# k0 ahead of the sketches, k1 and q1 between the halves of the weights, one outer product on GpSimd

## The chip, the core and the metric

The kernel runs on one core of a Trainium2 chip. A core has a matrix engine (TensorE, PE in the rows), three engines for element work (VectorE = DVE, ScalarE = ACT, GpSimd = POOL), a queue engine (SyncE = SP) that here only sends loads and stores, and 16 DMA engines. Each engine works through its own list of instructions in order; semaphores tie the lists together. The metric is the device time of one execution in microseconds, median over several runs. The list of each engine is exactly the order in which the Python code emits its instructions.

## What is computed

Linear attention with a polynomial feature map, then a feed-forward layer:

```python
def phi(x):                                   # x: (4 batches, 4 heads, 1088 tokens, 32)
    a = np.einsum('rd,bhsd->bhsr', S1, x)     # r = 8
    b = np.einsum('rd,bhsd->bhsr', S2, x)
    return np.einsum('bhsi,bhsj->bhsij', a, b).reshape(*x.shape[:-1], 64)
q_p, k_p = phi(q), phi(k)
kv  = np.einsum('bhsf,bhsd->bhfd', k_p, v)
z   = np.sum(k_p, axis=2)
num = np.einsum('bhsf,bhfd->bhsd', q_p, kv)
den = np.einsum('bhsf,bhf->bhs', q_p, z)[..., None] + 1e-06
x   = (num / den), as 4352 tokens x 128
h   = x @ w_in                                # 128 -> 2048
out = (h * sigmoid(beta * h)) @ w_out         # 2048 -> 128
```

The result is float32, 4352 x 128.

## The kernel before

The four batches go one after another through the attention part, and the feed-forward part is woven between its steps.

**Attention of a batch b.** `turn_k` and `turn_q` (DVE) transpose 32x32 blocks of the loaded k and q into `kT` and `qT`. `kps` (PE) multiplies `kT` by the sketches `sk` into PSUM; two DVE transposes bring that back as `kab`. `outer(b, h)` (DVE, one call per head) forms the 64 features of k in `kp`, out of two inputs in SBUF. `kv` (PE) multiplies `kp` by v and by ones, head by head within each j, into `kvz`; its first part takes j = 1 to 4, the second the rest. `ab` (PE) multiplies `qT` by the two sketches into `aps` and `bps`; ACT copies `aps` to `asb`, DVE multiplies `bps` by it into `qp`. `ndt` transposes `kv` and its sum (`zb`, `nd`). `den` and `num` (PE) give `dps` and `nps`; DVE inverts the denominator (`dT`, `rc`, `rb`) and writes the quotient into `xT`. q is handled in two parts n = 0 and 1 (18 and 16 of 34 blocks).

**Feed-forward.** Nine chunks of 512 tokens (the last of 256), eight waves each: `w1` is two PE products `wave` with `winp` and one ACT activation `g` (Silu) over 1024 columns; `w2` is two products into `moeout` with `woutp`, two waves behind. `winp` = w_in times beta and `woutp` = w_out divided by beta are made by GpSimd, in halves of 1024 columns of d_ff: four `prep_win`, four `prep_wout`, then again. `slot(group, n)` emits a step of attention and behind it n waves. So PE takes the waves and the attention steps in one fixed order: after the first three waves comes `ab` of batch 1 and batch 0 (`r_group((1, 0, 0), (0, 1, 1))`), which needs `qT` of batch 1. `keep_warm(n)` is n products on a tile of ones that no one reads.

**Loads.** Nearly all go through SP's queue in program order: S1, the first half of k0, q0; v0 (held behind the first `turn_k` of batch 0); w_in, beta (spread over the partitions), w_out, each of the first half and then each of the second; then k, q, v of batch 1, of 2, of 3. ACT's queue carries S2, the second half of k0 and a small copy of beta. A load of SP's that takes up a completion semaphore again waits for the load that used it last, so about eight loads are on the way at once.

The lines that matter below: the loads are L82 (S), L94 (k, q), L108 (v), L140, L141, L147 (w_in, beta, w_out); `turn_k` L307, `turn_q` L319, `kab` L341, `kp` L350, `qp` L392, `kvz` L410, `winp` L190, `woutp` L205.

Of the kernel before, what the change touches and what calls it, by code (L numbers as in the profile page):

```python
# [9 lines left out]
F32 = mybir.dt.float32  # L10
# [4 lines left out]
P = 128  # L15
# [3 lines left out]
def kernel(  # L19
# [58 lines left out]

    sr = []
    for n, (s_, eng) in enumerate(((S1, nc.sync), (S2, nc.scalar))):  # L80
        t = const.tile([P, D], F32, tag=f"sr{n}", name=f"sr{n}")
        eng.dma_start(  # L82
            out=t, in_=bass.AP(tensor=s_.tensor, offset=s_.offset, ap=[[0, P // R], [D, R], [1, D]])
        )
        sr.append(t)
# [45 lines left out]
    k_t[0] = load_rows(k, 0, "k", halves)  # L131
    q_t[0] = load_rows(q, 0, "q")
    nc.scalar.dma_start(out=beta_jp, in_=moe_beta.rearrange("(j p) -> j p", p=P))

    def load_rest(gate):
        v_t[0] = load_v(0, gate)
        for c in range(0, DFF, DFF // 2):
            cs = slice(c, c + DFF // 2)
            js = slice(c // P, (c + DFF // 2) // P)
            nc.sync.dma_start(out=w_in_sb[:, cs], in_=moe_w_in[:, cs])  # L140
            nc.sync.dma_start(  # L141
                out=beta_bc[:, cs],
                in_=bass.AP(
                    tensor=moe_beta.tensor, offset=moe_beta.offset + c, ap=[[0, P], [1, DFF // 2]]
                ),
            )
# [179 lines left out]
    def kps(b):  # L326
        t = ps2.tile([P, 2, 512], F32, tag="two", name="kps")
        for g in range(4):
            for pi in range(2):
                rows = slice(64 * pi, 64 * pi + 64)  # L330
                nc.tensor.matmul(  # L331
                    out=t[32 * g : 32 * g + 32, pi, : NJK * 32],
                    lhsT=sk[rows, :],
                    rhs=kT_of[b][rows, KBASE[g] * 32 : (KBASE[g] + NJK) * 32],
                    start=True,
                    stop=True,
                )

        KAB[b] = sbA.tile([P, 2, NJK, 32], F32, tag="kab", name="kab")
        for pi in range(2):  # L340
            nc.vector.transpose(  # L341
                out=KAB[b][:, pi].rearrange("p j c -> p (j c)"), in_=t[:, pi, : NJK * 32]
            )
        KP[b] = sbA.tile([P, H, NJK, F], F32, tag="kp", name="kp")

    def outer(b, h, j0=0, j1=NJK):
# [3 lines left out]
        nc.vector.tensor_tensor(  # L350
# [180 lines left out]


# [67 lines left out]
    for b in range(1, B + 1):  # L600
# [25 lines left out]
        if more:  # L626
            slot(lambda: kps(b + 1), two)
# [50 lines left out]
```

## Time and profile before

| | |
|---|---|
| time, median of 3 runs | 131.19 us (130.79 to 132.09) |
| the profiled execution | 129.78 us, its span 127.7 us |
| PE busy | 110.7 us (87% of the span) |
| ACT busy | 78.9 us (62%) |
| DVE busy | 67.9 us (53%) |
| GpSimd busy | 11.1 us (9%) |
| read from and written to HBM | 10.00 MB and 2.23 MB |
| mean granted clock of PE | 0.986 of full speed |

The span runs from the first to the last instruction of the execution; 2.08 us of its time lie around it. Busy time of PE counts pipelined products, so a busy PE need not be PE at its peak. In rows of the trace, "[0.67 <-DVE kp L350]" is idle time of the engine just before the row, and what ended it; "x8" counts instructions that the row merges.

### The profile page before, as it was taken

What the parts mean: (1) busy time and instruction counts of PE and PEld (TensorE: products, weight loads), DVE (VectorE), ACT (ScalarE), POOL (GpSimd) and SP (SyncE); (2) the same over time, 40 slices, a digit from 0 to 9 for tenths busy, and PEclk for the clock granted to TensorE, in tenths of its full rate; (3) what the DMA queues carried; (4) which work ended last, traced back from release to release, by engine and by line L of the source; (5) the groups of instructions that cost most, each with busy time, mean ns of one, the idle gap of its engine ahead of it and who ended that gap; (6) DMA issues with size and microseconds to landing.
All of it is one profiled execution on the core that took longest, in us unless ns stands there. A gap on an engine that the chain in (4) does not pass through costs nothing.

```text
span 127.7 us, 3100 instructions
## 1 busy us (share of the span) xinstructions
PE 110.7 (87%) x1282; PEld 45.6 (36%) x1282; DVE 67.9 (53%) x134; ACT 78.9 (62%) x96; POOL 11.1 (9%) x24
## 2 busy tenths in 40 slices
PE   5849979529959999969999999999999998989970
PEld 2224513112244423233433433453433343434550
DVE  2579326533892399899476589962449302020120
ACT  2303104704608666438798896688786899999960
POOL 3000399900000000000000000000000000000000
PEclk9999999995999999999999999999999999999999
DMA  2889999999980005000140004005000403203253
GB/s 43 319 187 274 334 354 381 216 308 220 306 185 19 11 9 78 0 0 0 26 63 0 5 10 72 0 5 82 0 5 11 71 0 53 29 6 47 37 79 44
DMA packets 24765, 12.42 MB, mean 97 GB/s; under 512 B 18976, under 2 KB 23088, under 8 KB 24752
## 3 DMA queue, kind: packets, MB, share of 16 engines
q1 hardware_dynamic: 23888, 11.88, 38.3%
q10 hardware_dynamic: 864, 0.35, 1.2%
q8 instruction: 10, 0.16, 0.6%
q14 instruction: 3, 0.02, 0.1%
HBM read 10.00 MB, written 2.23 MB: 96 GB/s over the span
## 4 chain that ended last, share of the span: by engine, by line
PE 45%; ACT 18%; DMA 12%; DVE 11%; SPq 8%; issue 4%; ACTq 0%; DVEq 0%
ACT g L269 17%; PE wave L261 15%; PE moeout L224 13%; DMA q<-in_q_dram 9%; PE kvz L410 4%; PE aps L373 4%; SPq L94 3%; DMA k<-in_k_dram 3%; PE dps L475 2%; PE nps L510 2%; DVE rb L493 2%; PE bps L373 2%; DVE kp L350 2%; PE kps L331 1%; DVE kT L307 1%
## 5 line engine op out<-in xcount | busy, mean ns | idle before, releaser
L269 ACT ACTIVATE g<-wave 128x1024 f16<-128x1024 f32 x68 | 65.5, 1033 | 17.9 <-PE wave L261 17.5
L261 PE MATMUL wave<-xT,winp 128*128 128x512 f16 (+1 forms) x144 | 40.9, 373 | 2.1 <-ACT g L269 1.0
L224 PE MATMUL moeout<-g,woutp 128*128 128x512 f16 (+1 forms) x144 | 39.4, 370 | 0.0
L261 PEld LDWEIGHTS <-winp 128*128 128x128 f16 x144 | 12.2, 97 | 23.5 <-issue 15.5
L224 PEld LDWEIGHTS <-woutp 128*128 128x128 f16 x144 | 14.2, 98 | 15.5 <-issue 0.8
L383 ACT COPY asb<-aps 128x576 f32<-128x576 f32 (+1 forms) x16 | 9.6, 613 | 15.5 <-PE aps L373 13.3
L234 DVE STREAM_TRANSPOSE o_sb<-moeout 128x512 f32<-128x512 f32 (+1 forms) x9 | 6.2, 687 | 23.2 <-PE moeout L224 23.2
L392 DVE TENSOR_TENSOR qp<-bps,asb 128x576 f32<-128x576 f32 (+1 forms) x16 | 11.3, 712 | 13.0 <-PE bps L373 8.7
L373 PE MATMUL aps<-qT,s_135 32*64 32x288 f32 (+1 forms) x128 | 11.3, 412 | 5.5 <-DVE qT L319 5.5
L373 PE MATMUL bps<-qT,s_140 32*64 32x288 f32 (+1 forms) x128 | 11.2, 411 | 0.3 <-ACT asb L383 0.3
L350 DVE TENSOR_TENSOR kp<-kab 128x576 f32<-128x576 f32 (+2 forms) x20 | 11.4, 617 | 0.0
L410 PE MATMUL kvz<-kp,v 128*32 128x64 f32 (+1 forms) x288 | 9.1, 223 | 2.4 <-DVE kp L350 2.4
L163 PE MATMUL warm<-idle 128*128 128x512 f16 x25 | 8.0, 458 | 1.5 <-DVE hm L175 1.5
L410 PEld LDWEIGHTS kvz<-kp,v 128*32 128x32 f32 (+1 forms) x288 | 6.2, 109 | 6.9 <-DVE kp L350 3.5
L373 PEld LDWEIGHTS aps<-qT,s_135 32*64 32x64 f32 x128 | 3.7, 129 | 10.7 <-issue 7.9
L307 DVE STREAM_TRANSPOSE kT<-k 128x1088 f32<-128x1088 f32 (+2 forms) x5 | 5.3, 1073 | 4.0 <-DMA k<-in_k_dram 4.0
L190 POOL TENSOR_TENSOR winp<-w_in_sb,beta_bc 128x256 f16<-128x256 f32 x8 | 5.6, 724 | 13.6 <-DMA beta_bc<-in_moe_beta_dram 13.6
L520 DVE TENSOR_TENSOR xT<-nps,rb 128x576 f16<-128x576 f32 (+1 forms) x8 | 5.8, 722 | 1.2 <-PE nps L510 1.0
L319 DVE STREAM_TRANSPOSE qT<-q 128x576 f32<-128x576 f32 (+1 forms) x8 | 5.8, 726 | 1.0 <-DMA q<-in_q_dram 1.0
L486 DVE STREAM_TRANSPOSE dT<-dps 128x288 f32<-128x288 f32 (+1 forms) x8 | 3.7, 461 | 5.0 <-PE dps L475 5.0
L493 DVE STREAM_TRANSPOSE rb<-rc 128x576 f32<-128x576 f32 (+1 forms) x8 | 6.0, 745 | 0.3
L510 PE MATMUL nps<-qp,nd 64*32 64x288 f32 (+1 forms) x128 | 5.5, 401 | 0.0
(53 smaller groups left out, 57.6 us busy)
## 6 DMA issues: line engine op xcount, KB each, us to landing
v<-in_v_dram SPq DMA_DIRECT2D x16, 144.0 KB, 8.1
q<-in_q_dram SPq DMA_DIRECT2D x4, 544.0 KB, 11.5
k<-in_k_dram SPq DMA_DIRECT2D x3, 544.0 KB, 11.9
out_dram<-o_sb SPq DMA_DIRECT2D x20, 64.0 KB, 2.0
w_in_sb<-in_moe_w_in_dram SPq DMA_DIRECT2D x2, 512.0 KB, 7.6
beta_bc<-in_moe_beta_dram SPq DMA_DIRECT2D x2, 512.0 KB, 8.2
w_out_sb<-in_moe_w_out_dram SPq DMA_DIRECT2D x2, 512.0 KB, 9.9
k<-in_k_dram SPq DMA_DIRECT2D x1, 288.0 KB, 3.7
```

The source lines that it names most:

```text
L163: nc.tensor.matmul(out=t, lhsT=idle[:, :P], rhs=idle, start=True, stop=True)
L224: nc.tensor.matmul(out=moe["acc"][:, :tw], lhsT=woutp[:, j, :], rhs=g[:, jj, :tw], start=(j == 0), stop=(j == NJ - 1),)
L261: nc.tensor.matmul(out=wv[:, jj * tw : (jj + 1) * tw], lhsT=winp[:, (j0 + jj) * P : (j0 + jj + 1) * P], rhs=xT[:, t0 : t0 + tw], start=Tru ...
L269: nc.scalar.activation(out=g, in_=wv, func=ACTF.Silu)
L307: last = nc.vector.transpose(out=kT_of[b][:, 32 * t0 : 32 * t1], in_=k_t[b][:, t0:t1].rearrange("p t d -> p (t d)"),)
L350: nc.vector.tensor_tensor(out=KP[b][:, h, j0:j1].rearrange("p j (i l) -> p j i l", i=R), in0=bass.AP(tensor=a0.tensor, offset=a0.offset, a ...
L373: nc.tensor.matmul(out=dst[64 * c : 64 * c + 64, m, : 32 * tn], lhsT=sx[rows, :], rhs=qT_of[bb][rows, t0 : t0 + tn, c, :], start=True, sto ...
L383: nc.scalar.copy(out=ASB[a_of][:, :, :w], in_=aps[:, :, :w])
L392: nc.vector.tensor_tensor(out=QP[bb][:, 2 * pr : 2 * pr + 2, 32 * t0 : 32 * t0 + w], in0=bps[:, :, :w], in1=ASB[b_of][:, :, :w], op=MUL,)
L410: nc.tensor.matmul(out=kvz[32 * h : 32 * h + 32, F * which : F * which + F], lhsT=v_t[b][:kr, h, j, :] if which == 0 else ones[:kr, :], rh ...
L493: nc.vector.transpose(out=rb[:, :tn].rearrange("p t c s -> p (t c s)"), in_=bass.AP(tensor=r0.tensor, offset=r0.offset, ap=[list(r0.ap[0]) ...
L510: nc.tensor.matmul(out=nps[32 * h : 32 * h + 32, c, :w], lhsT=ND[b][rows, 32 * h : 32 * h + 32], rhs=QP[b][rows, h, 32 * t0 : 32 * t0 + w] ...
```

## The change

**Loads.** The first half of k0 goes ahead of S1 on SP's queue, the second half ahead of S2 on ACT's. In the list of SP's loads k1 stands behind the first half of the weights, q1 behind w_in and beta of the second half, and w_out of the second half behind q1; v1 follows.

SP's queue before, from the first load of the weights to k and q of batch 1 (in the names, `in_..._dram` is the tensor in HBM):

```order
L140 DMA w_in_sb<-in_moe_w_in_dram 128x1024
L141 DMA beta_bc<-in_moe_beta_dram 128x1024
L147 DMA w_out_sb<-in_moe_w_out_dram 128x8x128
L140 DMA w_in_sb<-in_moe_w_in_dram 128x1024
L141 DMA beta_bc<-in_moe_beta_dram 128x1024
L147 DMA w_out_sb<-in_moe_w_out_dram 128x8x128
L94 DMA k<-in_k_dram 128x1088
L94 DMA q<-in_q_dram 128x1088
L108 DMA v<-in_v_dram 32x4x288 x4
```

And the same stretch of SP's queue now:

```order
L140 DMA w_in_sb<-in_moe_w_in_dram 128x1024
L141 DMA beta_bc<-in_moe_beta_dram 128x1024
L147 DMA w_out_sb<-in_moe_w_out_dram 128x8x128
L86 DMA k<-in_k_dram 128x1088
L140 DMA w_in_sb<-in_moe_w_in_dram 128x1024
L141 DMA beta_bc<-in_moe_beta_dram 128x1024
L86 DMA q<-in_q_dram 128x1088
L147 DMA w_out_sb<-in_moe_w_out_dram 128x8x128
L100 DMA v<-in_v_dram 32x4x288 x4
```

k1 is three loads further ahead, q1 one load; w_in and beta of the second half have k1 ahead of them, w_out has k1 and q1.

**The start on DVE.** The sketches are turned behind k0 (`load_rest` and `turn_k` stand ahead of them in the code), `qT` of batch 0 ahead of `kab`, and the reciprocal of beta behind all eight outer products of batch 0.

DVE before, from the first turned sketch on (`st` and `sk` are the sketches, `rbeta` the reciprocal of beta):

```order
L539 STREAM_TRANSPOSE st_132<-sr_81 128x32
L540 TENSOR_TENSOR sk<-st_132,hm 128x2x8
L539 STREAM_TRANSPOSE st_137<-sr_83 128x32
L540 TENSOR_TENSOR sk<-st_137,hm 128x2x8
L307 STREAM_TRANSPOSE kT<-k 128x576
L307 STREAM_TRANSPOSE kT<-k 128x512
L201 RECIPROCAL rbeta<-bt 128x16
L341 STREAM_TRANSPOSE kab<-kps 128x288 x2
L319 STREAM_TRANSPOSE qT<-q 128x576
L350 TENSOR_TENSOR kp<-kab 128x320 x4
L350 TENSOR_TENSOR kp<-kab 128x256 x4
```

And DVE now, from the same point:

```order
L316 STREAM_TRANSPOSE kT<-k 128x576
L316 STREAM_TRANSPOSE kT<-k 128x512
L555 STREAM_TRANSPOSE st_173<-sr_88 128x32
L556 TENSOR_TENSOR sk<-st_173,hm 128x2x8
L555 STREAM_TRANSPOSE st_178<-sr_90 128x32
L556 TENSOR_TENSOR sk<-st_178,hm 128x2x8
L328 STREAM_TRANSPOSE qT<-q 128x576
L354 STREAM_TRANSPOSE kab<-kps 128x288 x2
L364 TENSOR_TENSOR kp<-kab 128x320 x4
L364 TENSOR_TENSOR kp<-kab 128x256 x4
L210 RECIPROCAL rbeta<-bt 128x16
```

`kT` and the four sketch operations have changed places, `qT` has passed `kab`, and `rbeta` has gone to the end.

**Batch 1 on DVE.** `turn_k(1)` is emitted behind the multiplication of batch 0's second part.

DVE before, from the first quotient of batch 0 to `kab` of batch 1:

```order
L520 TENSOR_TENSOR xT<-nps,rb 128x2x9x32
L307 STREAM_TRANSPOSE kT<-k 128x1088
L392 TENSOR_TENSOR qp<-bps,asb 128x2x256
L319 STREAM_TRANSPOSE qT<-q 128x576
L392 TENSOR_TENSOR qp<-bps,asb 128x2x256
L341 STREAM_TRANSPOSE kab<-kps 128x288 x2
```

And now:

```order
L534 TENSOR_TENSOR xT<-nps,rb 128x2x9x32
L406 TENSOR_TENSOR qp<-bps,asb 128x2x256
L316 STREAM_TRANSPOSE kT<-k 128x1088
L328 STREAM_TRANSPOSE qT<-q 128x576
L406 TENSOR_TENSOR qp<-bps,asb 128x2x256
L354 STREAM_TRANSPOSE kab<-kps 128x288 x2
```

`kT` and the first `qp` have changed places; PE's order there is as it was.

**Heads and warm products.** In batches 1 to 3 `outer(b, 3)` runs on GpSimd, emitted right behind `kab`; before, DVE made it just ahead of `kv`. At the start the idle products ahead of the first part of `kv` are gone, two stand between its parts as before, and behind its second part stand one and two in place of two and three (21 in all, from 25). The diff, without the lines that only move or rename:

```diff
     k_t[0] = load_rows(k, 0, "k", halves)
+
+    sr = []
+    for n, (s_, eng) in enumerate(((S1, nc.sync), (S2, nc.scalar))):
...
     def load_rest(gate):
         v_t[0] = load_v(0, gate)
...
+        w_in_beta(0)
+        w_out(0)
+        k_t[1] = load_rows(k, 1, "k")
+        w_in_beta(hf)
+        q_t[1] = load_rows(q, 1, "q")
+        w_out(hf)
+        v_t[1] = load_v(1)
+        for b in range(2, B):
             k_t[b] = load_rows(k, b, "k")
...
-    def outer(b, h, j0=0, j1=NJK):
+        def evac():
+            for pi in range(2):
+                nc.vector.transpose(
+                    out=KAB[b][:, pi].rearrange("p j c -> p (j c)"), in_=t[:, pi, : NJK * 32]
+                )
+
+        return evac
+
+    def outer(b, h, j0=0, j1=NJK, eng=nc.vector):
...
-        nc.vector.tensor_tensor(
+        eng.tensor_tensor(
...
+    load_rest(turn_k(0, halves[:1]))
+    turn_k(0, halves[1:])
...
-    load_rest(turn_k(0, halves[:1]))
-    turn_k(0, halves[1:])
-    prep_rbeta()()
-    kps(0)
+    kps_evac = kps(0)
     turn_q(0, 0)
+    kps_evac()
     ab((0, 0, 0))
     mult00 = ab((0, 1, 0), (0, 0, 0))
     mult10 = ab(None, (0, 1, 0), (psm, "wave"))
+    recip = prep_rbeta()
     for h in range(H):
         outer(0, h, 0, 5)
-    keep_warm(2)
     kv(0, [1, 2, 3, 4])
-    keep_warm(2)
     for h in range(H):
         outer(0, h, 5, NJK)
+    recip()
+    keep_warm(2)
     mult00()
     mult10()
     kv(0, [5, 6, 7, 8, 0])
...
-    keep_warm(2)
     turn_q(0, 1)
+    keep_warm(1)
     ndt(0)
-    keep_warm(3)
+    keep_warm(2)
...
-    turn_k(1)
     slot(None, 2)
     slot(lambda: r_group(None, (0, 0, 1)), 1)
+    turn_k(1)
     turn_q(1, 0)
     slot(lambda: r_group((1, 0, 0), (0, 1, 1)), 1)
-    slot(lambda: kps(1), 1)
+    slot(lambda: kps(1)(), 1)
+    outer(1, 3, eng=nc.gpsimd)
     outer(1, 0)
...
             divide = num(b - 1, 1)
             if b < B:
-                outer(b, 3)
                 kv(b, [1, 2, 3, 4], None if b == 1 else 0)
...
-            slot(lambda: kps(b + 1), two)
+            slot(lambda: kps(b + 1)(), two)
+            outer(b + 1, 3, eng=nc.gpsimd)
             outer(b + 1, 0)
             outer(b + 1, 1)
```

## Rows read from the trace of the kernel before

**Rows 1.** Busy time by stage: window, its length, busy and count per engine, clock, DMA.

```profile
45.00:50.00 5.00, 4.63 (x51) 1.69 (x45) 5.00 (x10) 3.24 (x4) 0.00 (x0) 1.00 0.37 56
...
57.08:100.07 42.99, 42.24 (x486) 16.75 (x486) 29.22 (x53) 34.13 (x41) 0.00 (x0) 1.00 0.15 22
100.07:127.70 27.63, 23.03 (x116) 11.08 (x116) 3.29 (x5) 22.46 (x25) 0.00 (x0) 1.00 0.28 41
```

**Rows 2.** The chain that ended last: start, length, what it was.

```profile
11.71 3.72 SPq L94
15.47 11.37 DMA q<-in_q_dram
26.87 0.79 DVE qT L319
```

**Rows 3.** Busy time and clock around PE's idle stretches (columns as in Rows 1).

```profile
24.14:27.76 3.62, 0.00 (x1) 0.00 (x0) 2.46 (x3) 0.76 (x1) 1.27 (x3) 1.00 1.04 254
7.32:9.04 1.72, 0.00 (x0) 0.03 (x1) 1.65 (x4) 0.00 (x0) 0.00 (x0) 1.00 1.05 267
...
28.17:32.06 3.89, 3.89 (x38) 0.92 (x23) 1.30 (x3) 1.66 (x2) 0.00 (x0) 0.56 1.08 235
```

**Rows 4.** Timeline of SP's queue: start of the issue, its length, line, load.

```profile
1.46 0.81 SPq L94 DMA_DIRECT2D k<-in_k_dram  x1
...
8.76 0.43 SPq L147 DMA_DIRECT2D w_out_sb<-in_moe_w_out_dram  x1
...
11.08 0.58 SPq L147 DMA_DIRECT2D w_out_sb<-in_moe_w_out_dram  x1
...
16.92 2.31 SPq L108 DMA_DIRECT2D v<-in_v_dram  x4
```

**Rows 5.** Loads by window: both w_out in turn, then v1's last; KB, us to landing.

```profile
w_out_sb<-in_moe_w_out_dram SPq DMA_DIRECT2D x1, 512.0 KB, 8.8
...
w_out_sb<-in_moe_w_out_dram SPq DMA_DIRECT2D x1, 512.0 KB, 10.9
...
v<-in_v_dram SPq DMA_DIRECT2D x1, 144.0 KB, 10.4
```

**Rows 6.** Timeline of the start: start, busy, engine, line, operation, idle before.

```profile
3.15 0.21 DVE L539 STREAM_TRANSPOSE st_132<-sr_81 128x32 f32<-128x32 f32 x1 [1.26 <-DMA sr_81<-in_S_dram]
...
3.73 0.18 DVE L540 TENSOR_TENSOR sk<-st_137,hm 128x16 f32<-128x16 f32 x1
...
8.82 3.00 DVE L350 TENSOR_TENSOR kp<-kab 128x320 f32<-128x320 f32 x8
...
13.26 0.32 PE L410 MATMUL kvz<-kp,v 128*32 128x64 f32 x8
...
14.42 0.29 PE L410 MATMUL kvz<-kp,ones 64*32 64x64 f32 x8
...
22.37 0.66 PE L373 MATMUL bps<-qT,s_140 32*64 32x256 f32 x8
```

**Rows 7.** Timeline of DVE: `kT` and `qp` before `qT` of batch 1; heads of batch 2.

```profile
23.94 1.31 DVE L307 STREAM_TRANSPOSE kT<-k 128x1088 f32<-128x1088 f32 x1 [2.67 <-DMA k<-in_k_dram]
25.17 0.65 DVE L392 TENSOR_TENSOR qp<-bps,asb 128x512 f32<-128x512 f32 x1
...
48.09 1.39 DVE L350 TENSOR_TENSOR kp<-kab 128x576 f32<-128x576 f32 x2
```

**Rows 8.** Timeline of GpSimd: the second half of the weights.

```profile
20.35 2.78 POOL L190 TENSOR_TENSOR winp<-w_in_sb,beta_bc 128x256 f16<-128x256 f32 x4 [0.28 <-DMA beta_bc<-in_moe_beta_dram]
23.10 2.32 POOL L205 TENSOR_TENSOR woutp<-w_out_sb,rbeta 128x256 f16<-128x256 f32 x4
```

**Rows 9.** Timeline of PE: `kv` of batch 1, then of batch 2.

```profile
36.38 0.30 PE L410 MATMUL kvz<-kp,v 128*32 128x64 f32 x2 [0.37 <-DVE kp L350]
37.05 0.24 PE L410 MATMUL kvz<-kp,v 128*32 128x64 f32 x1 [0.37 <-DVE kp L350]
...
56.45 0.63 PE L410 MATMUL kvz<-kp,v 128*32 128x64 f32 x26 [1.04 <-DVE kp L350]
```

More of the change, by code (lines that the diff above doesn't have):

```diff
@@ L76 @@
     T0 = 2 * q_chk[0][1]
[L79 to L85, printed above, removed]
     beta_bc = const.tile([P, DFF], F32, tag="beta_bc")
@@ L131 @@
     k_t[0] = load_rows(k, 0, "k", halves)
+    sr = []
+    for n, (s_, eng) in enumerate(((S1, nc.sync), (S2, nc.scalar))):
+        t = const.tile([P, D], F32, tag=f"sr{n}", name=f"sr{n}")
+        eng.dma_start(
+            out=t, in_=bass.AP(tensor=s_.tensor, offset=s_.offset, ap=[[0, P // R], [D, R], [1, D]])
+        )
+        sr.append(t)
     q_t[0] = load_rows(q, 0, "q")
@@ L136, in load_rest, with w_in_beta, w_out @@
         v_t[0] = load_v(0, gate)
[L137 to L140, printed above, removed]
+        hf = DFF // 2
+        def w_in_beta(c):
+            nc.sync.dma_start(out=w_in_sb[:, c : c + hf], in_=moe_w_in[:, c : c + hf])
             nc.sync.dma_start(
[L142 to L145, printed above, removed]
+                out=beta_bc[:, c : c + hf],
+                in_=bass.AP(tensor=moe_beta.tensor, offset=moe_beta.offset + c, ap=[[0, P], [1, hf]]),
             )
+        def w_out(c):
             nc.sync.dma_start(
-                out=w_out_sb[:, js, :], in_=moe_w_out[cs, :].rearrange("(j p) m -> p j m", p=P)
-            )
-        for b in range(1, B):
+                out=w_out_sb[:, c // P : (c + hf) // P, :],
+                in_=moe_w_out[c : c + hf, :].rearrange("(j p) m -> p j m", p=P),
+            )
+        w_in_beta(0)
[6 more added lines that the diff above has]
+        for b in range(2, B):
             k_t[b] = load_rows(k, b, "k")
@@ L337, in kps @@
                 )
+        KP[b] = sbA.tile([P, H, NJK, F], F32, tag="kp", name="kp")
         KAB[b] = sbA.tile([P, 2, NJK, 32], F32, tag="kab", name="kab")
[L340 to L344, printed above, removed]
-    def outer(b, h, j0=0, j1=NJK):
+        def evac():
+            for pi in range(2):
+                nc.vector.transpose(
+                    out=KAB[b][:, pi].rearrange("p j c -> p (j c)"), in_=t[:, pi, : NJK * 32]
+                )
+        return evac
+    def outer(b, h, j0=0, j1=NJK, eng=nc.vector):
         a0 = KAB[b][:, h // 2, j0:j1, 2 * R * (h % 2) :]
@@ L570 @@
             prep_wout(j, j + 2)
+    turn_q(0, 1)
+    keep_warm(1)
+    ndt(0)
     keep_warm(2)
-    turn_q(0, 1)
-    ndt(0)
-    keep_warm(3)
     invert = den(0, 0)
```

## The prediction, made before the changed kernel ran

> **What bounds the kernel now.** I read the busy time by stage first, then the chain that ended last, then the timelines where the chain leaves the engines. From 57 us on, PE is busy in 42.24 of 42.99 us, and the last 27.63 us are a fixed run of waves on PE and ACT [rows 1]. Nothing of the change touches what is done there, so whatever is won before is kept to the end. The chain shows where time is lost ahead of that: SP sends k1 at 11.71 and q1 at 15.47, q1 is 11.37 us on its way and lands at 26.84, DVE turns it from 26.87 on [rows 2], and PE, which had nothing else in its order, sits from 24.14 to 27.76, 3.62 us without one product [rows 3]. Soon after it starts again the granted clock is low: 0.56 on average from 28.17 to 32.06, that is mostly the lower of the two levels, with PE busy throughout [rows 3]. So q1's landing is paid twice, once as idle time and once as slow products. An idle stretch of 1.72 us earlier on, from 7.32 to 9.04, left the clock at 1.00 [rows 3].
>
> **k1 and q1 ahead of weights.** The landings of before: first w_out 8.76 + 8.8 = 17.56, second w_out 11.08 + 10.9 = 21.98 [rows 4, 5], the second half of beta when GpSimd's wait for it ended, 20.35 [rows 8], k1 when DVE's wait ended, 23.94 [rows 7], q1 26.84. So w_in and beta of the second half took 2.79 us behind the first w_out, w_out 1.63, k1 1.96, q1 2.90. In the new order q1 has k1, w_in, beta and itself behind the first w_out: 17.56 + 1.96 + 2.79 + 1.96 = 24.27, with q1 as long as k1, its twin in size and form (the 2.90 had v1 mixed in, which now comes later). All loads behind v0 also start earlier: v0 is held behind the first `kT`, which waits for k0, sent at 1.46 [rows 4] and now at the head of the queue, at 0.73. That gives 23.54. Ends: 22.6, if k1 and q1 run like the weights (2.79 us per 1024 KB, so 1.48 for 544 KB); 25.2, if only the 1.63 us of w_out comes off. Issue is no limit: k1 and q1 left more than 10 us ahead of landing.
>
> Behind q1, `qT` takes 0.79 and PE follows 0.10 later (27.66 to 27.76): PE could start again at 24.4.
>
> **The start must keep up.** DVE's new order puts `qp` ahead of `kT`: with the start as it was, `bps` ends at 23.03 [rows 6], then 0.65, 1.31 [rows 7], 0.79 and 0.10 make 25.9. The start is earlier, though. k0 gains 0.73; the four sketch operations now follow `kT` and cost DVE what they took from 3.15 to 3.91, 0.76 [rows 6]; so the eight outer products end near 11.8, as before (8.82 + 3.00) [rows 6], if S lands in time behind k0; 0.7 either way are the ends. But `kv`'s second part began only at 13.26 and ended at 14.71 [rows 6], because PE had waited for `qT` behind `kab` and made idle products before and between. With `qT` ahead and two of those gone it can follow the heads, 1.4 us earlier; I take that, between 0 and 2.1. The restart by the start is then 24.5, the later of the two. **Gain: 27.76 - 24.5 = 3.3 us**, between 1.65 (q1 at 25.2) and 4.0 (heads 0.7 earlier, q1 no later than 22.9).
>
> Fewer idle products cost nothing by themselves; the reciprocal behind the heads is hidden, since GpSimd needs it only when the first w_out lands at 17.56. What the second half of the weights loses: beta lands at 20.35 + 1.96 - 0.73 = 21.6, w_out at 23.5 + 1.6 = 25.2, GpSimd is done at 25.2 + 2.32 = 27.5, before 25.4 [rows 8]. PE reaches these columns only after `kps` of batch 1, and their `woutp` two waves later; no cost.
>
> **The clock.** PE's idle stretch shrinks to 22.7 to 24.5, 1.8 us, close to the 1.72 that left the clock alone and far from the 3.62 that did not [rows 3]. The low stretch lost 3.89 x 0.44 = 1.7 us at most; some of it would have been waiting, so **1.5**, ends 0 and 1.7.
>
> **The fourth head on GpSimd.** In batch 1, `kv` got its third head at 36.38 and its fourth at 37.05 [rows 9]: the fourth off DVE is worth **0.7**. In batch 2 PE waited 1.04 for the head made last [rows 9]; DVE, full around it, saves one head: **0.7**, at most 1.04. Batch 3 shows no such wait: 0. On GpSimd, four products of 256 columns took 2.32 to 2.78 us [rows 8], so 576 columns take 1.3 to 1.6, an estimate. In batch 1 that ends near 29.1 behind the weights, and is wanted at 37.05 - 3.3 - 1.5 - 0.7 = 31.5. In batches 2 and 3 GpSimd is idle. No row shows DVE's outer products beside a GpSimd product: 0 if they don't meet, and up to 1.5 if the second outer product of batch 2 has to let the head pass, since DVE is busy in 5.00 of 5.00 us there [rows 1]. I take 0, because DVE's own products stand ready while GpSimd still waits for a semaphore. The Trainium skill (SBUF — State Buffer, "Who interferes with whom") says that a DVE instruction with two SBUF inputs and a GpSimd instruction that reads SBUF exclude each other for a whole instruction, the one that starts first going through; both kinds of outer product have two inputs in SBUF. By that rule the sum would be 1.5 smaller.
>
> **Sum:** 3.3 + 1.5 + 0.7 + 0.7 = 6.2 us. The profiled execution took 129.78 (127.7 of span and 2.08 around it) and would take 123.6. The median of before, 131.19, lies 1.41 above it; on that footing the forecast is **125.0**. What is late next is v1: its last part, sent by 18.9 and 10.4 us on its way [rows 4, 5], lands near 29, now perhaps 28.3, and `kv` of batch 1 wants it some 4.8 us earlier than before, near 30.
>
> **Rivals.**
> - *The clock falls all the same* (15%): PE has little to do in the whole start, and 1.8 us is not 1.72. Against it: the early stretch. 131.19 - 4.7 = 126.5.
> - *q1 is hardly earlier* (14%): q1's 2.90 us were not v1's doing, and only w_out's 1.63 us come off. For it: the landings show q1 slower than its twin. Restart at 26.1, 1.65 gained, PE idle over 3 us and the clock falls: 131.19 - 1.65 - 1.4 = 128.1.
> - *GpSimd's head and DVE's exclude each other* (11%): for it, DVE has no free time at 45 to 50; against it, DVE's heads may all start first. 131.19 - 4.7 = 126.5. This is the mechanism of the skill's rule above.
> - *GpSimd's head is far dearer than its weight products* (slower, 4%): both inputs repeat their elements, which no GpSimd row shows. Batch 1 decides: started at 27.5, behind the weights, it holds `kv` up from 4 us on (31.5) and makes it later than the old 37.05 from 9.5 us on. At 12 us `kv` of batch 1 would wait until 39.5, 2.5 later than before, and batch 2, which has 8.4 us from the first head at 48.09 [rows 7] to `kv` at 56.45 [rows 9], adds 3.6: 131.19 + 6.1 = 137.3. Against it: that is eight times the row's price.
> - *The change moves waits and no time* (6%): the start gains nothing, the clock falls, the head costs what it saves: within 1%.
>
> **Numbers.** The forecast's own case has 50% and runs from 123.6 (4.0 + 1.7 + 0.7 + 1.04 = 7.4 gained, rounded down) to 126. The range of 123.5 to 128.6 takes in the first three rivals. One per cent, 1.3 us, is about what a measurement of this kernel tells from no change. Faster by more: 50 + 15 + 14 + 11 = 90%; the same 6%; slower 4%.
>
> **What would show it.** In the profile after: q1 landing at 23 to 24.5, DVE's `qT` of batch 1 right behind it or behind `kT`, PE idle under 2.5 us there, the clock at 1.00 from 28 to 32 of the old timeline, `kv` of batch 1 and 2 no longer waiting for a fourth head of DVE, and GpSimd rows of about 1.5 us. I am wrong if q1 lands after 25, if a new wait for S, v1 or `woutp` stands ahead of PE, or if DVE's outer products grow beside GpSimd's.

## The result, and the profile after

The changed kernel took 127.44 us, the median of four executions, beside 131.64 us for the kernel before on the same chip: a ratio of 0.969, 95% interval 0.958 to 0.979. All ratios, here and below, leave disturbed executions out (here one of 545.5 us, beside three from 126.83 to 127.86), so they do not follow exactly from the medians beside them. That one was the profiled execution, so the rows here come from another run of the same unchanged code (128.32 us, ratio 0.977, 0.969 to 0.986; the profiled execution 128.23 us, its span 126.1).

The gain in the medians is 4.2 us both times, where 6.2 were forecast. First the loads that answer to [rows 2, 4, 5]: issues on SP's queue (start, length), then the same two loads with their us to landing.

```profile
8.47 0.87 SPq L86 DMA_DIRECT2D k<-in_k_dram  x1
...
11.76 0.80 SPq L86 DMA_DIRECT2D q<-in_q_dram  x1
```

```profile
k<-in_k_dram SPq DMA_DIRECT2D x1, 544.0 KB, 9.5
...
q<-in_q_dram SPq DMA_DIRECT2D x1, 544.0 KB, 11.6
```

k1 lands at 8.47 + 9.5 = 17.97 and q1 at 11.76 + 11.6 = 23.36; the forecast for q1 was 23.54. On DVE the wait for a load is gone [rows 2, 7], but `qp`, `kT` and `qT` of batch 1 now stand in one run behind the start:

```profile
24.97 0.69 DVE L406 TENSOR_TENSOR qp<-bps,asb 128x512 f32<-128x512 f32 x1 [3.68 <-ACT g L278]
25.58 1.30 DVE L316 STREAM_TRANSPOSE kT<-k 128x1088 f32<-128x1088 f32 x1
26.80 0.73 DVE L328 STREAM_TRANSPOSE qT<-q 128x576 f32<-128x576 f32 x1
...
32.17 0.57 DVE L502 TENSOR_SCALAR rc<-dT 128x16 f32<-128x16 f32 x1
...
46.51 2.37 DVE L364 TENSOR_TENSOR kp<-kab 128x576 f32<-128x576 f32 x2
```

The timeline of PE shows why that run is so late (it answers to [rows 6, 9]):

```profile
16.31 0.69 PE L489 MATMUL dps<-qp,zb 128*32 128x288 f32 x8 [0.52 <-ACT nd L482]
16.93 0.67 PE L524 MATMUL nps<-qp,nd 64*32 64x288 f32 x2
19.24 1.21 PE L524 MATMUL nps<-qp,nd 64*32 64x288 f32 x14 [1.64 <-issue]
...
23.22 1.03 PE L270 MATMUL wave<-xT,winp 128*128 128x512 f16 x4
...
27.69 0.42 PE L387 MATMUL aps<-qT,s 32*64 32x288 f32 x1 [1.74 <-DVE qT L328]
...
34.47 0.30 PE L424 MATMUL kvz<-kp,v 128*32 128x64 f32 x2 [1.06 <-DVE kp L364]
35.13 0.25 PE L424 MATMUL kvz<-kp,v 128*32 128x64 f32 x2 [0.37 <-DVE kp L364]
...
54.51 0.65 PE L424 MATMUL kvz<-kp,v 128*32 128x64 f32 x32
```

PE starts again at 27.69, only 0.10 us before the old 27.79. In the middle of `nps`, between two products of one group that share every input, it stood for 1.64 us with nothing to wait for that the profile shows ("issue"). The kernel before has a shorter stop of this kind, one step earlier:

```profile
16.59 0.69 PE L475 MATMUL dps<-qp,zb_123 128*32 128x288 f32 x6 [0.30 <-ACT nd L468]
17.92 0.64 PE L475 MATMUL dps<-qp,zb_123 128*32 128x288 f32 x2 [0.64 <-issue]
18.50 0.72 PE L510 MATMUL nps<-qp,nd 64*32 64x288 f32 x16
```

Last, the windows that answer to [rows 1, 3] (window, length, busy and count of PE, PEld, DVE, ACT, POOL, clock, DMA share, GB/s):

```profile
43.47:48.47 5.00, 4.51 (x44) 1.59 (x43) 4.88 (x8) 3.17 (x4) 1.54 (x1) 1.00 0.36 54
55.16:98.47 43.31, 42.17 (x486) 16.71 (x486) 30.18 (x54) 34.11 (x41) 1.51 (x1) 1.00 0.15 22
98.47:126.10 27.63, 22.95 (x116) 11.04 (x114) 3.29 (x5) 22.38 (x25) 0.00 (x0) 0.98 0.28 40
...
28.00:32.00 4.00, 4.00 (x51) 1.18 (x36) 2.50 (x5) 2.59 (x3) 1.93 (x3) 1.00 1.06 221
...
19.00:22.80 3.80, 3.56 (x35) 1.09 (x35) 0.76 (x1) 1.07 (x2) 2.15 (x4) 0.55 1.10 305
8.40:12.90 4.50, 4.49 (x94) 2.54 (x89) 4.50 (x12) 1.28 (x2) 0.00 (x0) 0.62 0.97 248
```

The stretch of low clock behind PE's restart [rows 3] is gone: 28 to 32 us is at 1.00 with PE busy throughout. Two others have come, at 8.4 to 12.9 and 19.0 to 22.8 us, both in the start, where the profile of before had none. Behind 55.16 us the changed kernel takes as long as before, but for 0.32 us more that the table below shows.

Stage by stage, from the two timelines of PE (before, after, gained; us):

| stage | before | after | gained |
|---|---|---|---|
| to the first `aps` of batch 1 | 27.79 | 27.69 | 0.10 |
| to `kps` of batch 1 | 2.35 | 1.67 | 0.68 |
| to `kps` of batch 2 | 16.02 | 15.27 | 0.75 |
| to the end of `kv`'s first part, batch 2 | 10.92 | 10.53 | 0.39 |
| to `kps` of batch 3 | 10.82 | 10.82 | 0.00 |
| to the end of `kv`'s first part, batch 3 | 12.50 | 12.74 | -0.24 |
| to the end | 47.30 | 47.38 | -0.08 |
| sum (span) | 127.70 | 126.10 | 1.60 |

So the profiled pair differs by 1.6 us, the medians by 4.2. The profiled execution of before was a good one: its clock was 0.986, where the 44 executions of that kernel beside the experiments had a median clock of 0.961 and a median time of 132.4 us.

### The profile page after: what moved, and what is told of

It is laid out like the page before. It is cut to its first block, busy times and chain, and to the rows that moved or that the text cites. A ratio compares the mean times of both kernels' runs of the same rounds, so it can differ in the third digit from the quotient of the medians.

```text
span 543.3 us, 3092 instructions
## 1 busy us (share of the span) xinstructions
PE 538.2 (99%) x1278; PEld 131.9 (24%) x1278; DVE 69.3 (13%) x131; ACT 83.9 (15%) x96; POOL 15.8 (3%) x27
## 4 chain that ended last, share of the span: by engine, by line
PE 99%; DVE 0%; issue 0%
PE moeout L233 33%; PE wave L270 33%; PE aps L387 7%; PE kvz L424 7%; PE warm L172 5%; PE nps L524 4%; PE dps L489 4%; PE bps L387 3%; PE kps L340 2%; PE ndps L469 1%; PE kvz L436 0%; DVE idle L167 0%; DVE o_sb L243 0%; PE bt L207 0%; DVE ones L176 0%
## 5 line engine op out<-in xcount | busy, mean ns | idle before, releaser
L233 PE MATMUL moeout<-g,woutp 128*128 128x512 f16 (+1 forms) x144 | 202.4, 1631 | 0.0
L270 PE MATMUL wave<-xT,winp 128*128 128x512 f16 (+1 forms) x144 | 194.4, 1572 | 0.0
L233 PEld LDWEIGHTS <-woutp 128*128 128x128 f16 x144 | 46.1, 320 | 127.4 <-issue 127.4
L270 PEld LDWEIGHTS <-winp 128*128 128x128 f16 x144 | 34.6, 255 | 138.1 <-issue 138.1
L387 PE MATMUL bps<-qT,s_181 32*64 32x288 f32 (+1 forms) x128 | 46.5, 1768 | 0.0
L387 PE MATMUL aps<-qT,s_176 32*64 32x288 f32 (+1 forms) x128 | 43.5, 1757 | 0.0
L424 PE MATMUL kvz<-kp,v 128*32 128x64 f32 (+1 forms) x288 | 30.3, 637 | 0.0
L172 PE MATMUL warm<-idle 128*128 128x512 f16 x21 | 28.4, 1655 | 1.5 <-DVE hm L184 1.5
L424 PE MATMUL kvz<-kp,ones 128*32 128x64 f32 (+1 forms) x144 | 20.0, 708 | 0.0
L489 PE MATMUL dps<-qp,zb_125 128*32 128x288 f32 (+1 forms) x32 | 11.5, 1626 | 0.0
L489 PE MATMUL dps<-qp,zb_123 128*32 128x288 f32 (+1 forms) x32 | 11.3, 1633 | 0.0
```

The source lines that it names most:

```text
L172: nc.tensor.matmul(out=t, lhsT=idle[:, :P], rhs=idle, start=True, stop=True)
L233: nc.tensor.matmul(out=moe["acc"][:, :tw], lhsT=woutp[:, j, :], rhs=g[:, jj, :tw], start=(j == 0), stop=(j == NJ - 1),)
L270: nc.tensor.matmul(out=wv[:, jj * tw : (jj + 1) * tw], lhsT=winp[:, (j0 + jj) * P : (j0 + jj + 1) * P], rhs=xT[:, t0 : t0 + tw], start=Tru ...
L387: nc.tensor.matmul(out=dst[64 * c : 64 * c + 64, m, : 32 * tn], lhsT=sx[rows, :], rhs=qT_of[bb][rows, t0 : t0 + tn, c, :], start=True, sto ...
L424: nc.tensor.matmul(out=kvz[32 * h : 32 * h + 32, F * which : F * which + F], lhsT=v_t[b][:kr, h, j, :] if which == 0 else ones[:kr, :], rh ...
L489: nc.tensor.matmul(out=dps[32 * h : 32 * h + 32, :w], lhsT=zb[b % 2][:, h, :], rhs=QP[b][:, h, 32 * t0 : 32 * t0 + w], start=True, stop=True,)
```

## The experiments

Two questions: what held the start up, and where the heads' 1.4 us went. For the first, the theory is that PE's own instructions came late: they are fetched by DMA, on a queue that the profile lists as "instruction", while the loads fill the DMA engines. Its rivals are that the loads were too late after all, that the new order of the start costs what it saves, and that the low clock alone did it. For the second: GpSimd's product excludes DVE's, against the idea that the fourth head was not awaited anyway. The first four kernels share one set of runs of before, the next four another, the three from "Both" on a third, and the last has its own. The second and the last set ran on other chips, so kernels of one set compare best.

**The changed kernel again.** No edit.

> The changed kernel once more, for a profile of an undisturbed execution and an interval. Theory A (the sum of the prediction: restart of PE at 24.5, clock held, both heads saved): 125.0 us, ratio 0.953. Theory B (the two outer products exclude each other where GpSimd's head meets DVE's, about 1.0 us for a pair of heads, and one of the other terms fails): 127.0 us, ratio 0.968. In B, DVE's pair of heads in batch 2 takes about 2.4 us in place of 1.39; in A 1.4.

128.32 us (127.46 to 128.97), ratio 0.977 (0.969 to 0.986): the run above. On the heads theory B was right: DVE's pair takes 2.37 us. The time is 1.3 us above B's.

**The old order of the loads.**

```diff
         w_in_beta(0)
         w_out(0)
+        w_in_beta(hf)
+        w_out(hf)
         k_t[1] = load_rows(k, 1, "k")
-        w_in_beta(hf)
         q_t[1] = load_rows(q, 1, "q")
-        w_out(hf)
```

> Order of the loads as before (w_in, beta, w_out of both halves, then k1, q1), all else as changed. If q1's landing is what the gain hangs on (A and B alike), q1 lands near 26, PE starts again near 27 and most of the gain is lost: the ratio to the kernel before is 0.98 to 1.0, and the clock falls again after the idle stretch. If the start and the heads make the gain, it stays near 0.97.

131.22 us (128.35 to 132.85), ratio 0.984 (0.964 to 1.005). The median gives back 2.9 of the 4.2 us; the interval is too wide to put a size on it. In the profile, which shows one of the longer executions (132.73 us), DVE's `kT` of batch 1 waits for k1 again, and PE, which starts again at 30.99, waits 5.3 us for `qT`:

```profile
28.67 1.31 DVE L316 STREAM_TRANSPOSE kT<-k 128x1088 f32<-128x1088 f32 x1 [3.22 <-DMA k<-in_k_dram]
```

So with the old order q1 sets the restart again. In the changed kernel, where `qT` waits for no load, it was something else that was late.

**The fourth head on DVE.**

```diff
-    outer(1, 3, eng=nc.gpsimd)
...
             if b < B:
+                outer(b, 3)
                 kv(b, [1, 2, 3, 4], None if b == 1 else 0)
...
-            outer(b + 1, 3, eng=nc.gpsimd)
```

> The fourth head of batches 1 to 3 back on DVE ahead of kv, all else as changed. Theory A: 1.4 us slower than the changed kernel (0.7 in batch 1, 0.7 in batch 2). Theory B (exclusion): within 0.5 us of the changed kernel, or faster, since what kv saves is lost on the heads that DVE has left.

128.69 us (126.83 to 131.47), ratio 0.979 (0.967 to 0.992), against 0.977 with the heads on GpSimd: no difference that can be measured. What happened shows in its timelines. DVE first, then PE:

```profile
45.30 1.38 DVE L364 TENSOR_TENSOR kp<-kab 128x576 f32<-128x576 f32 x2
```

```profile
52.31 0.31 PE L424 MATMUL kvz<-kp,v 128*32 128x64 f32 x6
53.66 0.63 PE L424 MATMUL kvz<-kp,v 128*32 128x64 f32 x26 [1.04 <-DVE kp L364]
```

The wait of 1.04 us for the last head is back [rows 9], and the pair of heads takes 1.38 us, where beside GpSimd's head it took 2.37: 0.99 us lost by DVE against one head saved. Measured between fixed points of PE, from `kps` on: with the head on GpSimd batch 1 has its last head 0.28 us sooner (5.77 against 6.05), batch 2 the first part of `kv` 0.46 sooner (10.53 against 10.99), batch 3 0.24 later (12.74 against 12.50). Together 0.5 us.

**The old start.** S ahead of k0, `kab` ahead of `qT`, `rbeta` early, 25 idle products; the rest as changed.

```diff
+    sr = []
+    for n, (s_, eng) in enumerate(((S1, nc.sync), (S2, nc.scalar))):
...
     k_t[0] = load_rows(k, 0, "k", halves)
 
-    sr = []
-    for n, (s_, eng) in enumerate(((S1, nc.sync), (S2, nc.scalar))):
...
     q_t[0] = load_rows(q, 0, "q")
...
-    load_rest(turn_k(0, halves[:1]))
-    turn_k(0, halves[1:])
...
+    load_rest(turn_k(0, halves[:1]))
+    turn_k(0, halves[1:])
+    prep_rbeta()()
+    kps(0)()
     turn_q(0, 0)
-    kps_evac()
...
```

> The start as before (S ahead of k0, kab ahead of qT, reciprocal early, 25 idle products), loads and heads as changed. Theory A: DVE's order qp, kT, qT lets PE start again at 25.8 where it was 24.5, so 1.3 us slower than the changed kernel, more if the clock falls. Rival: q1's landing alone sets the restart, so no difference (within 0.3 us).

130.29 us (127.7 to 131.45), ratio 0.976 (0.958 to 0.993). By the ratio the new start is worth nothing, by the median 2 us; its profile restarts PE at 28.23. Inconclusive on the size, but the stop is there too, four products earlier in the program, inside `dps`, as there are four more idle products:

```profile
20.26 0.64 PE L489 MATMUL dps<-qp,zb 128*32 128x288 f32 x2 [1.13 <-issue]
```

**Many small idle products.** The first ten products of `keep_warm` (512 columns each) become 84 of 64 columns and 5 of 512: 79 more products, which end at 7.74 us in the profile, where the ten ended at 5.69.

```diff
-    keep_warm(10)
+    t_s = pso.tile([P, TCH], F32, tag="moeout", name="warm")
+    for _ in range(84):
+        nc.tensor.matmul(out=t_s[:32, :64], lhsT=idle[:, :32], rhs=idle[:, :64], start=True, stop=True)
+    keep_warm(5)
```

> The changed kernel with its first 10 idle products (128x512) replaced by 84 small ones (32x64) and 5 large: 79 more pairs of PE instructions in the first 6 us. Theory C: PE's gap of 1.6 to 2.0 us ahead of nps is a fetch of instructions; it lay behind 220 recorded products in all five profiles, and its block is asked for some 128 products earlier and comes late behind the loads. With 79 pairs more at the start the request goes out near 5 to 6 us, the gap ahead of nps is gone, xT of batch 0 starts near 18.6 in place of 20.5 and PE restarts near 25.0: 1.5 to 2.5 us faster than the changed kernel, ratio 0.955 to 0.965. Rival D (the gap is a property of nps, or of the clock falling): the gap stays before nps, time as the changed kernel, ratio 0.975.

128.32 us (125.98 to 132.01), ratio 0.975 (0.966 to 0.985). The median did not move, so the 1.5 to 2.5 us that were expected did not come, though the best executions are faster (125.98, 126.5). In the profile of the fastest the stop in `nps` is gone and PE restarts where the prediction said. PE:

```profile
16.36 0.69 PE L492 MATMUL dps<-qp,zb 128*32 128x288 f32 x8 [0.52 <-POOL winp L202]
16.98 0.71 PE L527 MATMUL nps<-qp,nd 64*32 64x288 f32 x16
...
19.92 1.02 PE L273 MATMUL wave<-xT,winp 128*128 128x512 f16 x4 [0.21 <-DVE xT L537]
...
24.39 0.42 PE L390 MATMUL aps<-qT,s 32*64 32x288 f32 x1 [1.74 <-DVE qT L331]
...
38.84 0.64 PE L390 MATMUL bps<-qT,s 32*64 32x288 f32 x2 [1.08 <-issue]
```

`nps` runs through, and PE restarts at 24.39, where the prediction had 24.5. But a later stop is left, 1.08 us at the 601st recorded product, and one of 0.21 at the 474th. Two runs below that start with the same 89 products have both at the same two counts, up to 1.44 and 0.93 us long. So the small products take away the first stop and not the later ones.

A packet on the instruction queue q8 goes with the first stop (packets, MB, share). The profile does not name its engine; that it is PE's is inferred from the times. In the changed kernel one came between 17.0 and 17.2 us, 2 us before the stop ended, and none from the launch until then:

```profile
q8 instruction: 1, 0.02, 31.5%
```

In the kernel with small products one comes at 7.0 to 7.5 us, ahead of most loads:

```profile
q8 instruction: 1, 0.02, 16.4%
```

The Trainium skill (Runtime: NRT & Kernel Launch, "Instruction fetch mechanics") says that an engine's instructions are streamed in blocks of 16 KiB through a DMA queue of its own, and that crossing a block is mostly hidden. The packets of 0.02 MB agree with the first half; on the second the measurement decides: the first stop was 0.38 to 2.04 us in the kernel before and six others, and 5.39 us in one below.

**The same in the kernel before.** The same edit in the kernel before.

> The kernel before with the same start (84 small idle products and 5 large in place of 10). Theory C: its gap of 0.64 inside dps goes too, but q1 still lands near 26.8 and PE restarts near 27.7: no faster than 0.5 us, ratio 0.995 to 1.0. Rival D: the gap stays, ratio 1.0.

131.21 us (129.64 to 133.07), ratio 1.015 (1.005 to 1.024). The 0.64 us stop of before is gone there too, but PE waits for q1 in any case until 27.80, and the clock falls behind that wait (0.57 from 28 to 32). The products alone are no gain where q1 is the bound. Whether they cost anything is not settled: the ratio says 1.5% slower, the medians 0.8 us faster (131.21 beside 131.99).

**Three more idle products.** `keep_warm(13)` in place of `keep_warm(10)`, a control.

> Control for the small products: the changed kernel with 13 large idle products at the start in place of 10, so PE is as busy until 6.5 but has 3 pairs of instructions more, not 79. Theory C: the gap ahead of nps stays, 1.5 to 2 us long; time as the changed kernel within 0.5 us, ratio 0.97 to 0.98. If the clock at the start is what costs, it gains as much as the small products do.

128.26 us (126.07 to 130.0), ratio 0.980 (0.966 to 0.995). The stop stays, and it moves three products ahead in the program:

```profile
16.16 0.69 PE L489 MATMUL dps<-qp,zb 128*32 128x288 f32 x7 [0.52 <-ACT nd L482]
18.40 0.64 PE L489 MATMUL dps<-qp,zb 128*32 128x288 f32 x1 [1.55 <-issue]
...
22.80 1.03 PE L270 MATMUL wave<-xT,winp 128*128 128x512 f16 x4
```

Counted from the launch to the end of the stop, the changed kernel and this one have the same number of recorded products (first pair of PE, then PEld):

```profile
0.00:19.24 19.24, 14.06 (x221) 6.29 (x222) 11.26 (x34) 3.89 (x8) 5.50 (x16) 0.91 0.85 265
```

```profile
0.00:18.40 18.40, 12.62 (x221) 5.62 (x221) 9.68 (x30) 3.89 (x8) 3.20 (x12) 1.00 0.77 250
```

Before and every run so far with a stop have 220 or 221 there. The place is set by the number of PE's instructions, not by what the products are or wait for. The second line also answers the rival of the clock: it was at 1.00 up to the end of this stop and fell only then:

```profile
18.40:22.80 4.40, 4.40 (x40) 1.22 (x39) 2.46 (x5) 1.07 (x2) 4.00 (x7) 0.61 1.09 314
```

**GpSimd's head behind DVE's second.** In batches 2 and 3 the head on GpSimd is made to wait for DVE's second head.

```diff
-        eng.tensor_tensor(
+        return eng.tensor_tensor(
...
         if more:
             slot(lambda: kps(b + 1)(), two)
-            outer(b + 1, 3, eng=nc.gpsimd)
             outer(b + 1, 0)
-            outer(b + 1, 1)
+            last = outer(b + 1, 1)
+            behind(outer(b + 1, 3, eng=nc.gpsimd), last)
```

> In batches 2 and 3 GpSimd's head is made to wait until DVE has made its first two heads (a dependency, no work left out). Theory B (exclusion): DVE's pair of heads takes 1.39 us again in place of 2.37, and dps of batch 2 comes about 1 us earlier: 0.5 to 1.0 us faster than the changed kernel. Without exclusion: no difference, or slower if GpSimd's head is now late for kv.

127.27 us (126.28 to 127.95), ratio 0.983 (0.976 to 0.989): 1 us less in the median than the changed kernel in the other set, and the ratio not distinguishable. Timelines of DVE and of GpSimd:

```profile
46.94 1.39 DVE L364 TENSOR_TENSOR kp<-kab 128x576 f32<-128x576 f32 x2
...
49.20 1.06 DVE L364 TENSOR_TENSOR kp<-kab 128x576 f32<-128x576 f32 x1
```

```profile
48.47 1.18 POOL L364 TENSOR_TENSOR kp<-kab 128x576 f32<-128x576 f32 x1 [16.17 <-DVE kp L364]
```

The pair is back at 1.39 us, GpSimd's head takes 1.18 us in place of 1.54, and what it still meets is DVE's third head, 1.06 in place of 0.76. From `kps` to the end of `kv`'s first part: 9.54 us in batch 2 and 12.29 in batch 3, against 10.99 and 12.50 with all heads on DVE. With batch 1 (6.24 against 6.05, lost) that is 1.47 us. That this is the 1.4 of the forecast is luck: the forecast had 0.7 in batch 1 and nothing in batch 3. In batch 1, whose code is the changed kernel's, GpSimd was done with the weights later (30.65 against 29.04 us), and its head met DVE's first, 1.18 us long in place of 0.72. What the order of the two engines is worth shows in batch 2 beside the changed kernel: 9.54 against 10.53, so there the exclusion had taken 1 us.

**Both.** The small products and the head behind.

> The changed kernel with the 84 small and 5 large idle products at the start (as in the run with many small products) and with GpSimd's head of batches 2 and 3 held behind DVE's second head (as in the run with the head behind). Theory: the two stops are separate. The start gives PE its restart at 24 to 25 us, without a stop before or in nps, and the DVE pair of heads at batch 2 takes 1.4 us in place of 2.37, with dps of batch 2 waiting for less than 0.5 us. Expected 125.5 us, ratio to the kernel before 0.955 to 0.97. Rival: the heads are covered anyway once PE is earlier (GpSimd's turn then hides behind ACT's waves), and the time is that of the small products alone, ratio 0.975.

125.32 us (123.83 to 127.89), before beside it 132.68; ratio 0.951 (0.942 to 0.959). That is the best of all and what was expected (125.5). Its interval does not touch that of the changed kernel's second run (0.969 to 0.986), though in another set; it touches that of the first (0.958 to 0.979). Its profiled execution (127.68 us) restarts PE at 24.71 and has batch 2 as above (9.53 us); it lost time to the two later stops (0.93 and 1.44 us) and to a clock of 0.66 between 33 and 38 us.

**Both, with fewer idle products.** 70 small and 3 large ones, 73 in place of 89.

> As the run before it, with 70 small and 3 large idle products in place of 84 and 5: the idle products end about 1.4 us earlier (near 6.3 us), so that kps of batch 0 follows kT. Theory of the late instructions: what decides is how many products PE is given before the loads fill the DMA queues, and 73 do as well as 89: no stop at the 221st product, PE restarts 0 to 1 us earlier than with 89. Expected 125 us, ratio 0.95 to 0.97. Rival: the products mattered because they kept PE busy; with a longer idle stretch the granted clock falls before 20 us and the restart is no earlier than 26.

129.46 us (124.22 to 130.41), ratio 0.958 (0.942 to 0.973). The expectation that 73 do as well failed, and it is the best witness for the instructions. PE stops in the middle of batch 0's `kv`, 5.39 us long, and again at the 221st product; the packet comes between 15.6 and 15.8 us. Timeline, count and packet:

```profile
12.48 0.22 PE L427 MATMUL kvz<-kp,v 128*32 128x64 f32 x1
18.09 0.42 PE L427 MATMUL kvz<-kp,v 128*32 128x64 f32 x5 [5.39 <-issue]
```

```profile
0.00:18.08 18.08, 10.49 (x221) 6.83 (x221) 9.28 (x28) 3.25 (x6) 3.30 (x12) 0.96 0.82 255
```

```profile
q8 instruction: 1, 0.02, 30.4%
```

With 63 products more than the changed kernel, the 221st comes earlier in the program and in time (after 12.5 us, not 17.6), but its packet moves only 1.4 us earlier: the wait is longer. With 79 more the packet had been moved by 7.5 us and no stop came there. That the idle products keep PE busy is not what decides: these 73 end at 6.74 us, the 98 of the last run at 6.82 and the 89 of the next one at 6.61, and neither of these stops at the 221st. The profile shows one of the longer executions (130.41 us). Two of the six took 124.22 and 125.85, about as short as with 89 products, so the long stop may not come in every execution.

**Both, with batch 1's head on DVE.**

```diff
-    outer(1, 3, eng=nc.gpsimd)
...
+            if b == 1:
+                outer(1, 3)
```

> As the first of these three, and batch 1's fourth head on DVE again, just ahead of kv, as in the kernel before. In the changed kernel DVE's small rc operation took 0.57 us in place of 0.17 beside GpSimd's head of batch 1, and a head of DVE up to 1.18 in place of 0.72, so 0.4 to 0.9 us of the 0.7 that the head is worth go back. Expected: within 0.5 us of the first, kv of batch 1 waits 0.3 to 0.4 us for a DVE head. Rival: the head of batch 1 is worth its 0.7 us, and this one is that much slower.

127.18 us (124.93 to 131.01), ratio 0.964 (0.952 to 0.976), against 0.951 for both. The ranges overlap widely; from `kps` to the last head of batch 1 it took 6.50 us against 5.86, so the head of batch 1 on GpSimd looks worth its 0.6 us in this form. The expectation that most of it goes back to slowed DVE work was not borne out.

**Both, with 98 idle products.** 96 small and 2 large ones.

> As the run with both (89 idle products, head behind), with 96 small and 2 large idle products in place of 84 and 5: 98 products, 9 more, and they end about as early or earlier (near 6.8 us). In the runs with 89 the instructions of PE that are needed at the 221st recorded product were moved at 7 to 8 us, in the run with 73 only at 15.6 us, behind the loads. Theory: with more products ahead they are again moved by 8 us, there is no stop at the 221st product, PE restarts at 24 to 25 us, and the time is that of the run with both, 125.3 us within 1 us, ratio 0.945 to 0.965. Rival: 70 and 3 failed because the large products (5 against 3) hold PE longer, not because of their number; then 96 and 2 has the packet at 15 us or later again, a stop of 2 us or more, and a ratio of 0.965 or more.

128.5 us (127.0 to 130.86), ratio 0.973 (0.964 to 0.983): 3.2 us worse than the first of these four, which ran on another chip, and with the instructions early. The packet came between 6.0 and 6.5 us:

```profile
q8 instruction: 1, 0.02, 14.6%
```

There is no stop in `nps`, and the first wave starts at 19.34, so the rival about the large products falls. But now q1 is late: sent at 13.26 and 13.4 us on its way, where with 89 products it was sent at 13.12 and took 9.8. DVE and then the clock (two windows):

```profile
26.69 0.78 DVE L331 STREAM_TRANSPOSE qT<-q 128x576 f32<-128x576 f32 x1 [3.69 <-DMA q<-in_q_dram]
```

```profile
26.00:28.00 2.00, 0.38 (x8) 0.36 (x16) 0.78 (x1) 0.00 (x0) 1.22 (x2) 0.50 1.06 211
28.00:30.00 2.00, 2.00 (x19) 0.43 (x4) 0.69 (x1) 0.76 (x2) 0.04 (x1) 0.50 1.01 287
```

PE stands 5.55 us, the clock falls to its lower level, and q1 is paid twice as in the kernel before. So both halves of the expectation were tested: in the profiled execution the stop went as the theory says, and the time did not follow, because a second thing was late. Why q1 took 3.6 us longer in this execution is open.

## Why the prediction was right, and where it was not

**The time** lay in the range (127.44 in 123.5 to 128.6), with the forecast of 125.0 too low by 2.4 us. That it lay there is in part luck: in the profiled pair the largest term, the restart, gained 0.10 us of 3.3, and the pair differs by 1.6 us in all.

**What bounds the kernel** held: the part behind `kv` of batch 3 took 47.30 and 47.38 us, so a microsecond won ahead of it is a microsecond of the span.

**k1 and q1 ahead of weights** held: q1 at 23.36 against 23.54. k1 came 0.8 us earlier than the sum of landings gives (17.97 against 18.79). The rival "q1 is hardly earlier" falls for the profiled execution of the changed kernel. In the ten profiles with this order of the loads q1 landed between 22.9 and 26.7 us, and after 25, the prediction's own sign of being wrong, in two: with the head behind (25.91) and with 98 products (26.66).

**The start must keep up** is the step that failed. It took 1.4 us from an earlier second part of `kv` and set PE's restart at 24.5, the later of start and q1. The second part did begin earlier, but at 12.96 against 13.26, 0.3 us: the clock was 0.62 from 8.4 us on. With the heads on DVE, whose clock was at 1.00 there, it began at 11.79, the forecast's 1.4 us earlier:

```profile
11.79 0.32 PE L424 MATMUL kvz<-kp,v 128*32 128x64 f32 x8
```

Then came the stop of 1.64 us in `nps` where before had 0.64 in `dps`, and the low clock from 19.0 to 22.8. The first wave started at 23.22, against 21.41 before: 1.8 us later, not 1.4 earlier. So the step lacked a term, PE's instructions behind the loads. The trace of before held that term: a gap of 0.64 us put down to "issue" inside a group of equal products, which the prediction did not speak of. With the first stop gone and the clock at 1.00 the first wave started at 19.92 and PE's restart came at 24.39. That this is the forecast's 24.5 is luck again: there the second part began only at 13.01, and 1.29 us came from `dps` to `nps`, which took 1.91 us with the stop of before and 0.62 without.

How the loss divides shows from the start of `dps` to the first wave: 6.91 us in the changed kernel, 6.64 with three more idle products and 7.31 with the heads on DVE, against 3.56 with small products, without a stop. The stop itself is 1.64, 1.55 and 2.04 us of that; another 1.5 to 1.7 us were lost behind it, where the clock was 0.60 or 0.61 for 4 us. Not all of these are the clock's: before, where the clock stayed at 1.00, the same path took 4.82 us, 0.62 more than the stop of 0.64 explains. So about 1 us is the clock's, an estimate, and the stop is paid twice, as q1's landing was before.

**The clock** at the restart held in the changed kernel: PE idle 1.74 us, the clock 1.00 behind it. The same gap of 1.74 us came in seven other profiles, and in one of them, with 73 products, the clock behind it was 0.53 from 30.41 to 34 us. So likeness to the 1.72 us of [rows 3] was no sure ground, and in the changed kernel itself the stop of 1.64 us was followed by the low clock. The first stage behind the restart gained 0.68 and the next 0.75, with batch 1's head in it; 1.5 for the clock and 0.7 for the head were forecast, so 1.43 against 2.2.

**The fourth head on GpSimd.** Its price was right (1.18 to 1.69 us against 1.3 to 1.6), so the rival that has it far dearer falls. Its worth was wrong, 0.5 us in place of 1.4. GpSimd's rows in the changed kernel, with the weights of [rows 8] ahead of the heads of batches 1 and 2:

```profile
21.44 2.77 POOL L199 TENSOR_TENSOR winp<-w_in_sb,beta_bc 128x256 f16<-128x256 f32 x4 [1.65 <-DMA beta_bc<-in_moe_beta_dram]
26.71 2.33 POOL L214 TENSOR_TENSOR woutp<-w_out_sb,rbeta 128x256 f16<-128x256 f32 x4 [2.49 <-DMA w_out_sb<-in_moe_w_out_dram]
31.11 1.60 POOL L364 TENSOR_TENSOR kp<-kab 128x576 f32<-128x576 f32 x1 [2.07 <-DVE kab L354]
46.73 1.54 POOL L364 TENSOR_TENSOR kp<-kab 128x576 f32<-128x576 f32 x1 [14.03 <-DVE kab L354]
```

The prediction took nothing for the meeting, since DVE's heads would all start while GpSimd waits for a semaphore. But only the first one did: GpSimd started 0.22 us behind it, and the second then took 0.98 us more. That is the third rival's mechanism, at 0.98 us a pair and not 1.5. The Trainium skill (SBUF — State Buffer, "Who interferes with whom") has two such instructions exclude each other for a whole instruction, the one that starts first going through; the trace agrees (2.37 us in place of 1.39), and the run with GpSimd behind DVE turns it around (1.39 again). In batch 1 GpSimd's head met DVE's small `rc`, 0.57 us in place of the 0.17 that it took with the heads on DVE.

**No cost in the weights' second half** held: GpSimd was done at 29.0 (forecast 27.5), and no product of PE waits for it there, nor for v1.

**The footing.** The sum was made on a profiled execution whose clock was 0.986, and the difference to the median was added as a constant. Most executions of before had more low clock than that one; in the medians the change gained 4.2 us, in the profiled pair 1.6. The profiled execution of the changed kernel has two low stretches in the start, worth at most 4.50 x 0.38 and 3.80 x 0.45, 1.7 us each (an estimate); that of before has none there and one behind the restart. Where in the program the other 2.6 us lie is not shown, since only spans and mean clocks of those executions are known.

## What to carry to other kernels

Look at gaps called "issue" in the middle of a group of equal instructions: where the DMA engines are full, they can be an engine's own instructions arriving behind the loads, and moving work earlier can make them longer, if the packet does not move with it. When a wait on a load is shortened, work out anew what else ends at that time, and where two engines exclude each other, settle in the code which starts first: here that decided 1 us in batch 2. A gain that rests on one landing among many loads should be given a range from several executions, not from one profile.

## What the runs showed of the hardware that was not expected

- The stop of PE stood at the 220th or 221st recorded product in every kernel that had it, over four starts with 21, 24, 25 and 84 idle products, and ended 2.0 to 2.5 us after an instruction packet (15.4 to 17.92 in before, 17.0 to 19.24, 16.0 to 18.46 with the heads on DVE, 15.6 to 18.09 with 73 products). Later stops stood at the 474th and the 601st, 254 and 381 behind the 220th: 0.20 to 0.93 and 1.08 to 1.44 us in the three profiles with 89 products and the new start, and 0.29 and 0.50 us at the 474th in the changed kernel and with three more.
- The granted clock fell at places that differ from execution to execution: 8.4 to 12.9 and 19.0 to 22.8 in the changed kernel (0.62 and 0.55), 10 to 15 with the old start (0.66), 35 to 38 with the head behind (0.56), nowhere from 8 to 38 in the profiled execution with small products (1.00 in each of six windows of 5 us). One place recurs: right at the first stop's end in the changed kernel, with three more idle products, with the heads on DVE (0.60 or 0.61 for 4 us) and with 73 products (0.53 from 17 to 24), though not behind the stops of 0.38 to 1.13 us in the other four.
- One load of 544 KB took 9.8 to 14.3 us from issue to landing in kernels that sent it in the same order.
